# Batch 0's k and v by head halves, two early w_in tiles, and small products joined to the next k times v

## The chip, the cores and the metric

The kernel runs on one core of one Trainium2 chip. The metric is the device time of one execution in microseconds (us); the median of three runs of the kernel before is 1548.06. The core has a matrix engine (TensorE, here PE, with its weight loads PEld), VectorE (DVE), ScalarE (ACT), GpSimd (POOL) and SyncE (SP), whose queue issues nearly all DMAs.

## The reference

Three stages follow each other; q, k, v and the result are f32:

```
kv  = einsum('bhsd,bhse->bhde', k, v)          # 8 batches, 8 heads, 576 rows, head size 64
o   = einsum('bhsd,bhde->bhse', q, kv)
x   = o / sqrt(mean(o*o, -1) + 1e-6) * g_norm  # then (8*576 = 4608 tokens, 512)
x   = (s * relu(x @ w_in1)**2 + b) @ w_out1    # hidden size 2048
h   = x @ w_in2;  out = (h * sigmoid(h)) @ w_out2
```

The weight matrices arrive as f64, which the kernel reads as pairs of 32-bit words and decodes into f32 parts.

## The kernel before

All work is laid out by a planner (class `Plan`, method `run`). Each step is added with a price for each engine that could do it, a key (its due time in units), what it needs, makes, takes and gives, and, for a DMA, its time on the bus (`move`). The planner runs a clock of its own and at each point gives the free engine the ready step with the smallest key; this fixes the order of instructions on each engine for good. On the chip an engine waits for whatever its next instruction needs, and all that stands behind it in its queue waits too. `DMA_START`, `DMA_END` and the rates set how the planner reckons a DMA's landing. A unit is one of the 16 slices of 128 hidden columns of one block of 512 tokens: 12 products into `h` and 12 into `acc`, each 512 columns wide; wide products are made three at a time from high and low halves (`mm3`). Until 40 us of the planner's clock, PE's free time is filled with products of zeros (`warm_up`, line 1321).

A block is a batch's first 512 rows; the 64 remaining rows of the eight batches make a ninth. Attention goes by pairs of heads (`attention_pair(bb, p, key, before)`): 4 pairs in each of 8 batches. `kv` multiplies k by v in one burst of products into one PSUM bank: four chunks of 128 rows and one of 64 remaining rows (in a tile padded with zeros), for each of two heads, with the heads in the two halves of the output's partitions and so in two halves of 64 weight columns. `o` multiplies q by it, `rem` does so for the 64 remaining rows (line 566), `sq` and `part` square and sum in parts, `ms` adds the parts up over partitions on PE (line 640), `rms`, `inv`, `spread` and `x` norm the block. `rem` and `ms` are lone f32 products of 128 weight columns, each in a PSUM bank of its own. The tiles `kv`, `rem`, `q` and `qT` of later batches have one buffer each. `o` of a pair needs the x of the pair before it (`prev`), and the burst needs that pair's remaining rows to be copied out (`prev_r`).

Batch 0 (`z`) borrows the space of weight tiles that are not yet decoded (`wtag`). Its k and v come as 128 partitions of four rows of each head, and the remaining rows of all eight heads in two loads of their own (`load_rem`, 128 KB each, rows of 256 bytes) that the first burst waits for. Its q is turned by products with the identity (`q0_turn`, line 501).

`decode` reads one weight tile (`load`, 512 KB for a whole tile of layer 1) and makes its high and low parts: `mag`, `carry`, `hi` on ACT, `sign`, `top`, `lo` on DVE, `total` on POOL. The first two w_in tiles have keys -5 and -4.8, after all loads of batch 0, whose keys are -15, -13, -11 and -9 by pair.

From line 1303 on the pairs get their keys and are added in the order of them; blocks 1 to 4 are worked in plain units, the rest later in pairs of blocks with seven products in place of eight (`hidden`, `outputs`).

Of the kernel before, what the change touches and what calls it, by code (L numbers as in the profile page):

```python
# [8 lines left out]
F32 = mybir.dt.float32  # L9
# [10 lines left out]
class Plan:  # L20
# [10 lines left out]
    PE_START = 1.1  # L31

# [7 lines left out]
    def add(self, engines, key, fn, needs=(), makes=(), takes=(), gives=(), move=None, opens=(), until=None):  # L40
        self.ops.append((key, len(self.ops), engines, fn, needs, makes, takes, gives, move, opens, until))
        for b in gives:
            self.users[b] = self.users.get(b, 0) + 1

    def run(self):
# [41 lines left out]
        while done < len(self.ops):  # L87
# [46 lines left out]
def kernel(  # L134
# [148 lines left out]
    def decode(layer, kind, m, c, width, sfx, key, needs=(), quarter=None, made=()):  # L283
# [153 lines left out]
    def lend(tag):  # L437
        return f32(wp.tile([P, 2, DM], F32R, tag=tag, name=f"lent_{tag}"))
# [9 lines left out]
    def attention_pair(bb, p, key, before=None):  # L448
# [13 lines left out]
        rr = slice(REM, 2 * REM) if z else slice(REM)  # L462

        def kv_tile(e):
            st["kv"] = lend(wtag["kv"]) if z else ap.tile([P, 2, 2 * T // P * D], F32, tag="kv", name="kv", bufs=1)
# [11 lines left out]
        def load_rem(i):  # L477
            def go(e):
                dst, h = (lent["rem"], slice(0, H)) if z else (rem_t, hh)
                dma(  # L480
                    dst[:REM, i].rearrange("p (h d) -> p h d", d=D), (k, v)[i][bb, h, T:, :].rearrange("h p d -> p h d")
                )
# [12 lines left out]
        def q0_turn(e):  # L495
            lent["z", p] = lend_flat(wtag["qT"], 2 * DM)
            st["psq"] = psum(b["psq"], "q_ps")
            t = st["q"].rearrange("p (h c d) -> p h c d", h=2, d=D)
# [24 lines left out]
        def kv(e):  # L523
            pk = st["psk"] = psum(b["psk"], "kv_ps")
            t = st["kv"].rearrange("p i (h c d) -> p i h c d", h=2, d=D)
            t2 = lent["rem"][:, :, 2 * p * D:2 * (p + 1) * D] if z else rem_t
            for c in range(NCH + 1):
                for j in range(2):
                    jj = slice(j * D, (j + 1) * D)
                    kk = t[:, 0, j, c, :] if c < NCH else t2[:, 0, jj]  # L530
                    vv = t[:, 1, j, c, :] if c < NCH else t2[:, 1, jj]
                    nc.tensor.matmul(pk[jj, :D], kk, vv, start=(c == 0), stop=(c == NCH))  # L532

# [14 lines left out]
        def q0_out(e):  # L548
            copy(e, lent["z", p][:, :T].rearrange("p (t c) -> p t c", t=P), st["psq"].rearrange("p (c t) -> p t c", t=P))
# [36 lines left out]
        fr = (0, 0) if z else me  # L586

        prev, prev_r = ([], []) if z else ([("x32",) + before], [("ro",) + before])
        add({"PE": 0.73}, key, kv, needs=[f("k"), f("v"), ("kr",) + fr, ("vr",) + fr] + prev_r, makes=[f("kv")],
            takes=[b["psk"]], gives=[b["kv"], ("wo12", 0) if z else b["rem"]])  # L590
        add({ACT: 0.21, DVE: 0.26}, key + 0.3, kv_out, needs=[f("kv")] + ([("kvf0L",)] if z else []), makes=[f("kvf")],
            takes=[b["kvf"]], gives=[b["psk"]])
        if z:
            add({"PE": 0.5}, key + 0.2, q0_turn, needs=[f("q")], makes=[f("qt")], takes=[b["psq"], b["qT"]], gives=[b["q"]])
            add({ACT: 0.56}, key + 0.25, q0_out, needs=[f("qt")], makes=[f("q32")], gives=[b["psq"]])
            add({"PE": 0.95}, key + 1.5, o, needs=[f("kvf"), f("q32")], makes=[f("o")], takes=[b["pso"]])
# [13 lines left out]
        add({"PE": 0.2}, key + 2.2, rem, needs=[f("kvf"), f("qT")], makes=[f("r")], takes=[] if z else [b["psr"]],  # L610
            gives=[b["kvf"], b["qT"]])
# [4 lines left out]
        normalize(bb, p, key + 2, [f("o")], [b["pso"]] + [b["qT"]] * z, lambda: st["pso"])  # L616

    def normalize(t, p, key, needs, gives, src):
# [5 lines left out]
        psm = ("at", ("m", me))  # L624
# [13 lines left out]
        def ms(e):  # L638
            st["ps"] = psum(psm, "m_ps")
            nc.tensor.matmul(st["ps"][:, :T // Q], pairs_of, st["part"], start=True, stop=True)  # L640

        def rms(e):
            st["rms"] = ap.tile([P, T // Q], F32, tag="rms", name="rms", bufs=2)
            nc.scalar.activation(st["rms"], st["ps"][:, :T // Q], AF.Sqrt, bias=eps, scale=1.0 / D)
# [20 lines left out]
        add({"PE": 0.2}, key + 0.4, ms, needs=[f("part")], makes=[f("ms")], takes=[psm], gives=[("part", me)])  # L665
# [524 lines left out]
    with tc.manual_schedule():  # L1190
# [8 lines left out]
        lent["rem"] = lend("wo12")  # L1199
        nc.vector.memset(lent["rem"][REM:], 0.0)  # L1200
# [177 lines left out]
```

## Time and profile before

| | us |
|---|---|
| runs | 1549.67, 1547.32, 1548.06 |
| profiled execution | 1549.24 |
| its span | 1547.5 |
| PE busy | 1536.7 |
| granted TensorE clock, mean | 0.998 |

The span is what the trace covers; the execution's time includes some 1.7 us around it. PE is busy nearly throughout, also with the fillers, so its busy time alone does not tell useful work. An f32 product shows as two records; wide products are one record each. The end of a record is modelled and overlaps the next record, so distances between starts are the measure on PE.

### The profile page before, as it was taken

The numbers are of one execution on the slowest core, as the hardware profiler recorded it, in microseconds if no ns is written. First come the engines' busy times: TensorE is split into PE (matmuls) and PEld (weight loads), VectorE is DVE, ScalarE is ACT, GpSimd is POOL, SyncE is SP. The second block draws the span as 40 slices with busy tenths as digits, with TensorE's granted clock in tenths as the row PEclk, the third lists the DMA queues.
The fourth block names the chain that finished last, engine by engine and source line by source line (L and its number), as shares of the span: only waits on it lengthen the run. The fifth ranks groups of instructions, "written<-read, shape, count | busy, mean of one in ns | idle before, by whom it ended". The sixth has DMA issues, their size and how long they took to land.

```text
span 1547.5 us, 23039 instructions
## 1 busy us (share of the span) xinstructions
PE 1536.7 (99%) x7402; PEld 1255.4 (81%) x7402; DVE 1084.1 (70%) x1908; ACT 855.9 (55%) x1683; POOL 634.4 (41%) x584
## 2 busy tenths in 40 slices
PE   9999999999999999999999999999999999999999
PEld 6778888887888888888888788888888888888887
DVE  6887787877677587888888766765676666666521
ACT  6886566566576586667665444544444344544222
POOL 2331122111125144578457823762376246622410
PEclk9999999999999999999999999999999999999999
DMA  8866789988466788897988876877677766876684
GB/s 220 214 188 197 218 253 285 280 233 243 164 217 231 254 254 261 281 310 249 333 277 289 259 239 192 264 189 252 190 258 189 250 196 218 189 254 200 198 197 150
DMA packets 343496, 361.22 MB, mean 233 GB/s; under 512 B 166480, under 2 KB 228944, under 8 KB 343376
## 3 DMA queue, kind: packets, MB, share of 16 engines
q1 hardware_dynamic: 343248, 359.76, 76.4%
q8 instruction: 59, 0.97, 0.3%
q14 instruction: 61, 0.50, 0.1%
q0 software_dynamic: 128, 0.00, 0.0%
HBM read 272.63 MB, written 87.03 MB: 232 GB/s over the span
## 4 chain that ended last, share of the span: by engine, by line
PE 88%; DMA 4%; DVE 3%; ACT 2%; SPq 1%; issue 1%; POOL 1%; POOLq 0%; ACTq 0%; DVEq 0%
PE hp L980 28%; PE acc L1121 10%; PE acc L1123 10%; PE acc L1122 10%; PE h L208 5%; PE h L210 4%; PE h L209 4%; PE acc L208 4%; PE acc L209 4%; PE acc L210 4%; DMA raw<-in_moe_w_out_dram 1%; PE kv_ps L532 1%; PE acc L820 1%; PE acc L819 1%; PE acc L821 1%; SPq L236 1%
## 5 line engine op out<-in xcount | busy, mean ns | idle before, releaser
L980 PE MATMUL hp<-xo,win 128*128 128x512 f32 x2016 | 510.6, 390 | 1.8 <-DVE tmp L1005 1.8
L980 PEld LDWEIGHTS hp<-xo,win 128*128 128x128 f32 x2016 | 378.0, 188 | 84.1 <-DVE tmp L1005 5.9
L220 POOL TENSOR_TENSOR g<-tmp,g 128x512 fp32r<-128x512 f32 x192 | 249.7, 1308 | 309.4 <-ACT g L214 277.7
L1121 PE MATMUL acc<-g,wout 128*128 128x512 f32 x672 | 262.0, 390 | 0.8 <-DVE ya L1132 0.5
L1123 PE MATMUL acc<-g,wout 128*128 128x512 f32 x672 | 261.8, 390 | 0.0
L1122 PE MATMUL acc<-g,wout 128*128 128x512 f32 x672 | 261.7, 389 | 0.0
L1130 DVE TENSOR_TENSOR ya<-acc,ya 128x512 f32<-128x512 f32 x168 | 115.6, 688 | 126.9 <-PE acc L1123 117.8
L1121 PEld LDWEIGHTS acc<-g,wout 128*128 128x128 f32 x672 | 126.1, 188 | 27.9 <-DVE ya L1132 0.9
L1123 PEld LDWEIGHTS acc<-g,wout 128*128 128x128 f32 x672 | 126.3, 188 | 26.4
L1122 PEld LDWEIGHTS acc<-g,wout 128*128 128x128 f32 x672 | 126.3, 188 | 26.2
L214 ACT ACTIVATE g<-tmp 128x512 fp32r<-128x512 f32 x192 | 119.4, 629 | 26.3 <-PE acc L1123 11.7
L208 PE MATMUL acc<-gh,wo 128*128 128x512 f32 x320 | 132.2, 413 | 0.4 <-ACT y L227 0.4
L786 ACT ACTIVATE h<-h 128x512 f32<-128x512 f32 x96 | 56.0, 583 | 131.9 <-PE h L210 131.3
L208 PE MATMUL h<-xh,wi 128*128 128x512 f32 x320 | 126.7, 396 | 0.1
L1157 POOL TENSOR_TENSOR ya<-ya 128x512 f32<-128x512 f32 x84 | 108.2, 1318 | 45.1 <-DVE ya L1130 35.6
L210 PE MATMUL h<-xh,wi 128*128 128x512 f32 x320 | 125.2, 391 | 0.0
L210 PE MATMUL acc<-gh,wo 128*128 128x512 f32 x320 | 125.2, 391 | 0.0
L209 PE MATMUL acc<-gh,wo 128*128 128x512 f32 x320 | 125.1, 391 | 0.0
L209 PE MATMUL h<-xl,wi 128*128 128x512 f32 x320 | 124.9, 390 | 0.0
L332 POOL TENSOR_TENSOR rq<-raw 128x256 uint32<-128x256 uint32 x68 | 43.5, 640 | 189.5 <-DVE raw L318 101.1
L1005 DVE TENSOR_TENSOR tmp<-hp,tmp 128x512 f32<-128x512 f32 x144 | 98.8, 686 | 24.5 <-PE hp L980 23.1
L214 ACT ACTIVATE rq<-rq 128x256 fp32r<-128x256 f32 x192 | 77.5, 413 | 63.4 <-POOL rq L332 28.9
(170 smaller groups left out, 2649.4 us busy)
## 6 DMA issues: line engine op xcount, KB each, us to landing
wout<-wo SPq DMA_DIRECT2D x368, 256.0 KB, 4.2
win<-wi SPq DMA_DIRECT2D x144, 512.0 KB, 5.1
wi<-rq SPq DMA_DIRECT2D x96, 256.0 KB, 3.7
wo<-rq SPq DMA_DIRECT2D x96, 256.0 KB, 3.4
win<-wi SPq DMA_DIRECT2D x80, 256.0 KB, 4.2
raw<-in_moe_w_out_dram SPq DMA_DIRECT2D x36, 256.0 KB, 4.2
raw<-in_moe_w_in_dram SPq DMA_DIRECT2D x16, 512.0 KB, 4.8
raw<-in_moe_w_in_dram SPq DMA_DIRECT2D x32, 256.0 KB, 4.8
```

Of the source, the lines that this page charges most:

```text
L208: nc.tensor.matmul(ps, wh, xh, start=first, stop=False)
L209: nc.tensor.matmul(ps, wh, xl, start=False, stop=False)
L210: nc.tensor.matmul(ps, wl, xh, start=False, stop=last)
L214: nc.scalar.activation(hi, src, AF.Copy)
L220: eng[e].tensor_tensor(lo, src, f32(hi), op=ALU.subtract)
L980: nc.tensor.matmul(to, w[:, wn, f_], x_[:, xn], start=first and n == 0, stop=kk == KH - 1 and n == 2, skip_group_check=True)
L1005: nc.vector.tensor_tensor(t, bank[me, a], tmp[b_, me], op=ALU.add)
L1121: nc.tensor.matmul(to, w[:, 0, dd], gh, start=a == 0, stop=False)
L1122: nc.tensor.matmul(to, w[:, 0, dd], gl, start=False, stop=False)
L1123: nc.tensor.matmul(to, w[:, 1, dd], gh, start=False, stop=a == 1)
L1130: nc.vector.tensor_tensor(y2[tp, i, d], st["ps"], y2[tp, i, d], op=ALU.add)
L1157: eng[e].tensor_tensor(y2[tp, i, d], y2[tp, i, d], y2[tp, j, d], op=ALU.add)
```

## The change

It does five things. (1) Batch 0's k and v are loaded with a head in 64 partitions, nine rows in each, so the remaining rows come with them and `load_rem` is gone for batch 0; its burst becomes nine chunks of 64 rows for each head. Its q is loaded in the same way (eight rows in a partition) and turned in 16 products of 64 columns in place of 8 of 128. (2) The loads of the first two w_in tiles get keys -13.5 and -11.5. (3) For later pairs `rem` and `ms` are no longer steps: `kv` of the next pair issues them at its end, each as two products of 64 weight columns, into columns 64 to 143 of its own bank. The burst now needs the pair's `kvf`, `qT` and `part`. The last pair and batch 0 keep the lone form. (4) Pairs of batches 2 to 4 get other keys. (5) The planner reckons DMAs that are issued before 9 us at 1.2 times their length and with 1.8 us at the end, and some steps have other prices.

```diff
+    EARLY, EARLY_RATE, EARLY_END = 9.0, 1.2, 1.8
...
-                dma = max(dma, end + self.DMA_START) + op[8] * (self.BUSY_RATE if busy else 1.0)
-                end = dma + (self.DMA_BUSY if busy else self.DMA_END)
+                early = end < self.EARLY
+                dma = max(dma, end + self.DMA_START) + op[8] * (self.BUSY_RATE if busy else self.EARLY_RATE if early else 1.0)
+                end = dma + (self.DMA_BUSY if busy else self.EARLY_END if early else self.DMA_END)
...
-        first = layer == 0 and (kind, m) == ("i", 0)
-        add({"SP": 0.48}, -5 if first else key - 5 - 0.8 * (layer == 0 and (kind, m) == ("i", 1)), load, needs=needs, makes=[f(0)], takes=[raw], move=width * P * 8 / 3.6e5)
-        key -= 0.5 if first else 0.5
+        add({"SP": 0.48}, {(0, "i", 0): -13.5, (0, "i", 1): -11.5, (0, "o", 0): -3.4}.get((layer, kind, m), key - 5), load, needs=needs, makes=[f(0)], takes=[raw], move=width * P * 8 / 3.6e5)
+        key -= 0.5
...
+    bursts, joined = {}, {}
+
+    def attention_pair(bb, p, key, before=None, after=None):
...
-        wtag = {"kv": f"wo{8 + p}", "q": f"wo{4 + p}", "qT": f"wi{11 + p}", "kvf": "kvf0L"}
+        wtag = {"kv": f"wo{8 + p}", "v": f"wi{9 - p}", "q": f"wo{4 + p}", "qT": f"wi{11 + p}", "kvf": "kvf0L"}
         b = {n: (wtag[n] if z else n, me) for n in ("kv", "rem", "q", "qT") if not (z and n == "rem")}
+        if z:
+            b["v"] = (wtag["v"], me)
...
+        host = ("at", ("k", after)) if after else None
+        if after:
+            b["psr"] = host
+        rr = slice(REM, 2 * REM) if z or after else slice(REM)
...
+        def load_rows(i):
+            def go(e):
+                t = st["kv"[i]] = lend_flat(wtag[("kv", "v")[i]], S)
+                dma(t, (k, v)[i][bb, hh].rearrange("h (p c) d -> (h p) (c d)", p=D))
+            return go
...
-            st["q"] = lend_flat(wtag["q"], 2 * T // P * D)
-            dma(
-                st["q"].rearrange("p (h c d) -> p h c d", h=2, d=D), q[bb, hh, :T, :].rearrange("h (p c) d -> p h c d", p=P)
-            )
+            st["q"] = lend_flat(wtag["q"], T)
+            dma(st["q"], q[bb, hh, :T, :].rearrange("h (p c) d -> h p (c d)", p=D))
...
-            for c in range(NCH):
+            for c in range(T // D):
+                cc = slice(c * D, (c + 1) * D)
                 for j in range(2):
-                    nc.tensor.matmul(st["psq"][j * D:(j + 1) * D, c * P:(c + 1) * P], t[:, j, c, :], ident, start=True, stop=True)
+                    jj = slice(j * D, (j + 1) * D)
+                    nc.tensor.matmul(st["psq"][jj, cc], st["q"][jj, cc], ident[jj, jj], start=True, stop=True)
...
+            if z:
+                n = S // D
+                for c in range(n):
+                    cc = slice(c * D, (c + 1) * D)
+                    for j in range(2):
+                        jj = slice(j * D, (j + 1) * D)
+                        nc.tensor.matmul(pk[jj, :D], st["k"][jj, cc], st["v"][jj, cc], start=(c == 0), stop=(c == n - 1))
+                return
...
+            bursts[me] = pk
+            for more in joined.get(before, ()):
+                more()
...
+            if after:
+                st["psr"] = bursts[after]
+                for jj in (slice(D), slice(D, P)):
+                    nc.tensor.matmul(st["psr"][jj, rr], st["kvf"][:, jj], st["qT"][:, T:], start=True, stop=True)
+                return
...
-        add({"SP": 0.48}, lk, load(0), makes=[f("k")], opens=[f("kvo")], takes=[b["kv"]], move=0.73)
-        add({"SP": 0.48}, lk, load(1), needs=[f("kvo")], makes=[f("v")], move=0.73)
-        if not z or p == 0:
-            rb = ("wo12", 0) if z else b["rem"]
-            add({"SP": 0.63}, lk, load_rem(0), makes=[f("kr")], opens=[f("remo")], takes=[rb], move=0.73 if z else 0.18)
-            add({"SP": 0.63}, lk, load_rem(1), needs=[f("remo")], makes=[f("vr")], move=0.73 if z else 0.18)
+        if z:
+            for i in range(2):
+                add({"SP": 0.48}, lk, load_rows(i), makes=[f("kv"[i])], takes=[b[("kv", "v")[i]]], move=0.82)
+        else:
+            add({"SP": 0.48}, lk, load(0), makes=[f("k")], opens=[f("kvo")], takes=[b["kv"]], move=0.73)
+            add({"SP": 0.48}, lk, load(1), needs=[f("kvo")], makes=[f("v")], move=0.73)
+            add({"SP": 0.63}, lk, load_rem(0), makes=[f("kr")], opens=[f("remo")], takes=[b["rem"]], move=0.18)
+            add({"SP": 0.63}, lk, load_rem(1), needs=[f("remo")], makes=[f("vr")], move=0.18)
...
-        add({"PE": 0.73}, key, kv, needs=[f("k"), f("v"), ("kr",) + fr, ("vr",) + fr] + prev_r, makes=[f("kv")],
-            takes=[b["psk"]], gives=[b["kv"], ("wo12", 0) if z else b["rem"]])
+        more = before in joined
+        if more:
+            prev_r = [(x,) + before for x in ("kvf", "qT", "part")]
+        add({"PE": 1.2 if z else 0.93 + 0.24 * more}, key, kv, needs=[f("k"), f("v")] + ([] if z else [f("kr"), f("vr")]) + prev_r,
+            makes=[f("kv")] + ([(x,) + before for x in ("r", "ms")] if more else []), takes=[b["psk"]],
+            gives=[b["kv"], b["v"] if z else b["rem"]] + ([(f"kvf{before[1] % 2}", before), ("qT", before), ("part", before)] if more else []))
...
+            add({"PE": 1.0}, key + 0.2, q0_turn, needs=[f("q")], makes=[f("qt")], takes=[b["psq"], b["qT"]], gives=[b["q"]])
...
+            add({"PE": 1.1}, key + 1.5, o, needs=[f("kvf"), f("q32")], makes=[f("o")], takes=[b["pso"]])
...
-        add({"PE": 0.2}, key + 2.2, rem, needs=[f("kvf"), f("qT")], makes=[f("r")], takes=[] if z else [b["psr"]],
-            gives=[b["kvf"], b["qT"]])
+        if after:
+            joined[me] = [lambda: rem("PE")]
+        else:
+            add({"PE": 0.25}, key + 2.2, rem, needs=[f("kvf"), f("qT")], makes=[f("r")], takes=[] if z else [b["psr"]],
+                gives=[b["kvf"], b["qT"]])
...
+        psm = ("at", ("k", after) if after else ("m", me))
+        mc = slice(P, P + T // Q) if after else slice(T // Q)
...
+            if after:
+                st["ps"] = bursts[after]
+                for jj in (slice(D), slice(D, P)):
+                    nc.tensor.matmul(st["ps"][jj, mc], pairs_of[:, jj], st["part"], start=True, stop=True)
+                return
...
-        add({"PE": 0.2}, key + 0.4, ms, needs=[f("part")], makes=[f("ms")], takes=[psm], gives=[("part", me)])
+        if after:
+            joined[me].append(lambda: ms("PE"))
+        else:
+            add({"PE": 0.23}, key + 0.4, ms, needs=[f("part")], makes=[f("ms")], takes=[psm], gives=[("part", me)])
...
-        lent["rem"] = lend("wo12")
-        nc.vector.memset(lent["rem"][REM:], 0.0)
...
-        seq = [(t, p, KF * (t - 1) + (0.5 + (3.2 if t < LB else 2.0) * p if t > 1 else 0.75 + 3.4 * p)) for t in range(1, TP) for p in range(NP)]
+        seq = [(t, p, KF * (t - 1) + (-2 + (3.7 if t < LB else 2.0) * p if t > 1 else 0.75 + 3.4 * p)) for t in range(1, TP) for p in range(NP)]
...
-        for t, p, key in sorted(seq, key=lambda c: c[2]):
-            attention_pair(t, p, key, before)
+        seq.sort(key=lambda c: c[2])
+        for n, (t, p, key) in enumerate(seq):
+            attention_pair(t, p, key, before, seq[n + 1][:2] if n + 1 < len(seq) else None)
```

## Rows read from the trace of the kernel before

**Rows 1.** The page, busy us (share of the span) xinstructions of each engine

```profile
PE 1536.7 (99%) x7402; PEld 1255.4 (81%) x7402; DVE 1084.1 (70%) x1908; ACT 855.9 (55%) x1683; POOL 634.4 (41%) x584
```

**Rows 2.** Windows: length; PE, PEld, DVE, ACT, POOL busy (records); clock, DMA share, GB/s

```profile
0.00:27.00 27.00, 24.55 (x252) 18.26 (x253) 14.05 (x36) 13.47 (x32) 5.45 (x15) 1.00 0.91 237
...
45.00:430.00 385.00, 383.23 (x2173) 308.78 (x2171) 300.33 (x630) 255.00 (x569) 84.45 (x104) 1.00 0.77 227
...
840.00:880.00 40.00, 37.58 (x157) 29.96 (x156) 30.29 (x49) 18.31 (x37) 33.22 (x32) 0.96 0.82 262
```

**Rows 3.** Windows of line L1321, the fillers: PE and PEld busy (xrecords)

```profile
0.00:27.00 27.00, 13.14 (x91) 9.72 (x91) 1.00 0.91 237
27.00:45.00 18.00, 5.49 (x41) 3.27 (x39) 1.00 0.75 196
```

**Rows 4.** Timeline of PE at a k times v burst: start, us, what

```profile
121.08 0.39 PE L210 MATMUL acc<-gh,wo 128*128 128x512 f32 x1
121.40 0.69 PE L532 MATMUL kv_ps<-kv 128*64 128x64 f32 x16
121.92 0.29 PE L532 MATMUL kv_ps<-rem_t 128*64 128x64 f32 x4
...
122.47 0.39 PE L209 MATMUL acc<-gh,wo 128*128 128x512 f32 x1
```

**Rows 5.** Timeline of PE at a product for the remaining rows

```profile
69.74 0.39 PE L210 MATMUL h<-xh,wi 128*128 128x512 f32 x1
69.97 0.33 PE L566 MATMUL r_ps<-qT,kvf 128*128 128x64 f32 x2
...
70.42 0.40 PE L209 MATMUL acc<-gh,wo 128*128 128x512 f32 x1
```

**Rows 6.** Timeline of PE at a product for the mean squares

```profile
140.24 0.39 PE L210 MATMUL h<-xh,wi 128*128 128x512 f32 x1
140.47 0.29 PE L640 MATMUL m_ps<-part,pairs_of 128*128 128x16 f32 x2
140.61 0.50 PE L208 MATMUL h<-xh,wi 128*128 128x512 f32 x1
140.94 0.40 PE L209 MATMUL h<-xl,wi 128*128 128x512 f32 x1
```

**Rows 7.** Lines of PE: remaining rows of later pairs, xrecords | busy, mean ns

```profile
L566 PE MATMUL r_ps<-qT,kvf 128*128 128x64 f32 x56 | 9.3, 247 | 0.0
```

**Rows 8.** Timeline of all engines, 289 to 296 us: one later pair's chain

```profile
289.44 0.29 PE L640 MATMUL m_ps<-part,pairs_of 128*128 128x16 f32 x2
...
292.08 0.74 DVE L659 SCALAR_TENSOR_TENSOR x<-o_ps,vecs,sq 128x512 f32<-128x512 f32 x1
...
295.39 0.70 DVE L633 TRANSPOSE_TENSOR_REDUCE part<-sq 128x16 f32<-128x512 f32 x1
```

**Rows 9.** Waits of PE, 45 to 430 us: total, times, longest

```profile
PE m_ps L640 <- DVE orem L233: 0.8, 2, 0.6
```

**Rows 10.** Timeline of PE in the start

```profile
5.65 0.97 PE L532 MATMUL kv_ps<-lent_wo 128*64 128x64 f32 x16
7.76 0.34 PE L532 MATMUL kv_ps<-lent_wo 128*64 128x64 f32 x4 [1.14 <-DMA lent_wo<-in_v_dram]
...
18.33 1.09 PE L501 MATMUL q_ps<-ident,lent_wo 128*64 128x128 f32 x16
```

**Rows 11.** Windows in the start, columns as in rows 2

```profile
3.00:8.00 5.00, 3.86 (x33) 2.64 (x31) 0.83 (x5) 0.00 (x0) 2.16 (x8) 1.00 0.77 203
...
14.00:19.00 5.00, 5.00 (x59) 3.30 (x57) 3.06 (x6) 3.41 (x11) 0.00 (x0) 1.00 1.09 348
...
15.70:31.00 15.30, 15.30 (x134) 11.79 (x133) 14.38 (x29) 11.90 (x25) 2.40 (x2) 1.00 0.90 228
```

**Rows 12.** Timeline of DVE: a decode pass, pair 3's x

```profile
22.26 0.66 DVE L318 SCALAR_TENSOR_TENSOR raw<-dw,raw 128x512 uint32<-128x512 uint32 x1
...
29.92 0.69 DVE L220 TENSOR_TENSOR xl<-x,xh 128x512 fp32r<-128x512 f32 x1 [0.35 <-ACT xh L214]
```

More of the change, by code (lines that the diff above doesn't have):

```diff
@@ L446 @@
     lent = {}
-    def attention_pair(bb, p, key, before=None):
+    bursts, joined = {}, {}
+    def attention_pair(bb, p, key, before=None, after=None):
         me = (bb, p)
@@ L461, in attention_pair @@
         b["psq"] = ("acc", ("q", me))
-        rr = slice(REM, 2 * REM) if z else slice(REM)
+        host = ("at", ("k", after)) if after else None
+        if after:
+            b["psr"] = host
+        rr = slice(REM, 2 * REM) if z or after else slice(REM)
         def kv_tile(e):
-            st["kv"] = lend(wtag["kv"]) if z else ap.tile([P, 2, 2 * T // P * D], F32, tag="kv", name="kv", bufs=1)
+            st["kv"] = ap.tile([P, 2, 2 * T // P * D], F32, tag="kv", name="kv", bufs=1)
+        def load_rows(i):
[3 more added lines that the diff above has]
+            return go
         def load(i):
@@ L478, in go @@
             def go(e):
-                dst, h = (lent["rem"], slice(0, H)) if z else (rem_t, hh)
                 dma(
-                    dst[:REM, i].rearrange("p (h d) -> p h d", d=D), (k, v)[i][bb, h, T:, :].rearrange("h p d -> p h d")
+                    rem_t[:REM, i].rearrange("p (h d) -> p h d", d=D), (k, v)[i][bb, hh, T:, :].rearrange("h p d -> p h d")
                 )
@@ L497, in q0_turn @@
             st["psq"] = psum(b["psq"], "q_ps")
-            t = st["q"].rearrange("p (h c d) -> p h c d", h=2, d=D)
-            for c in range(NCH):
+            for c in range(T // D):
+                cc = slice(c * D, (c + 1) * D)
                 for j in range(2):
-                    nc.tensor.matmul(st["psq"][j * D:(j + 1) * D, c * P:(c + 1) * P], t[:, j, c, :], ident, start=True, stop=True)
+                    jj = slice(j * D, (j + 1) * D)
+                    nc.tensor.matmul(st["psq"][jj, cc], st["q"][jj, cc], ident[jj, jj], start=True, stop=True)
         def q0_rem_turn(e):
@@ L524, in kv @@
             pk = st["psk"] = psum(b["psk"], "kv_ps")
+            if z:
[6 more added lines that the diff above has]
+                return
             t = st["kv"].rearrange("p i (h c d) -> p i h c d", h=2, d=D)
-            t2 = lent["rem"][:, :, 2 * p * D:2 * (p + 1) * D] if z else rem_t
             for c in range(NCH + 1):
@@ L529, in kv @@
                     jj = slice(j * D, (j + 1) * D)
-                    kk = t[:, 0, j, c, :] if c < NCH else t2[:, 0, jj]
-                    vv = t[:, 1, j, c, :] if c < NCH else t2[:, 1, jj]
+                    kk = t[:, 0, j, c, :] if c < NCH else rem_t[:, 0, jj]
+                    vv = t[:, 1, j, c, :] if c < NCH else rem_t[:, 1, jj]
                     nc.tensor.matmul(pk[jj, :D], kk, vv, start=(c == 0), stop=(c == NCH))
+            bursts[me] = pk
+            for more in joined.get(before, ()):
+                more()
         def kv_out(e):
@@ L548, in q0_out @@
         def q0_out(e):
-            copy(e, lent["z", p][:, :T].rearrange("p (t c) -> p t c", t=P), st["psq"].rearrange("p (c t) -> p t c", t=P))
+            copy(e, lent["z", p][:, :T].rearrange("p (t c) -> p t c", t=D), st["psq"].rearrange("p (c t) -> p t c", t=D))
         def q_hi(e):
@@ L585, in attention_pair @@
                 opens=[f("qo")] * (i == 0), takes=[b["q"]] * (i == 0), move=0.42)
-        fr = (0, 0) if z else me
         prev, prev_r = ([], []) if z else ([("x32",) + before], [("ro",) + before])
-        add({"PE": 0.73}, key, kv, needs=[f("k"), f("v"), ("kr",) + fr, ("vr",) + fr] + prev_r, makes=[f("kv")],
-            takes=[b["psk"]], gives=[b["kv"], ("wo12", 0) if z else b["rem"]])
+        more = before in joined
[4 more added lines that the diff above has]
+            gives=[b["kv"], b["v"] if z else b["rem"]] + ([(f"kvf{before[1] % 2}", before), ("qT", before), ("part", before)] if more else []))
         add({ACT: 0.21, DVE: 0.26}, key + 0.3, kv_out, needs=[f("kv")] + ([("kvf0L",)] if z else []), makes=[f("kvf")],
@@ L593, in attention_pair @@
         if z:
-            add({"PE": 0.5}, key + 0.2, q0_turn, needs=[f("q")], makes=[f("qt")], takes=[b["psq"], b["qT"]], gives=[b["q"]])
+            add({"PE": 1.0}, key + 0.2, q0_turn, needs=[f("q")], makes=[f("qt")], takes=[b["psq"], b["qT"]], gives=[b["q"]])
             add({ACT: 0.56}, key + 0.25, q0_out, needs=[f("qt")], makes=[f("q32")], gives=[b["psq"]])
-            add({"PE": 0.95}, key + 1.5, o, needs=[f("kvf"), f("q32")], makes=[f("o")], takes=[b["pso"]])
+            add({"PE": 1.1}, key + 1.5, o, needs=[f("kvf"), f("q32")], makes=[f("o")], takes=[b["pso"]])
             add({"PE": 0.2}, key + 2.1, q0_rem_turn, needs=[("qr0",), f("kvf"), ("mm1o", 1, KD - 1)], makes=[f("qrt")], takes=[b["psr"]], gives=[("wo13", 0)])
@@ L615, in attention_pair, with normalize @@
             makes=[f("orem")], gives=[b["orem"]], move=0.18)
-        normalize(bb, p, key + 2, [f("o")], [b["pso"]] + [b["qT"]] * z, lambda: st["pso"])
-    def normalize(t, p, key, needs, gives, src):
+        normalize(bb, p, key + 2, [f("o")], [b["pso"]] + [b["qT"]] * z, lambda: st["pso"], after)
+    def normalize(t, p, key, needs, gives, src, after=None):
         z = t == 0
@@ L623, in normalize @@
         f = lambda name: (name, t, p)
-        psm = ("at", ("m", me))
+        psm = ("at", ("k", after) if after else ("m", me))
+        mc = slice(P, P + T // Q) if after else slice(T // Q)
         def sq(e):
@@ L638, in ms @@
         def ms(e):
+            if after:
[3 more added lines that the diff above has]
+                return
             st["ps"] = psum(psm, "m_ps")
-            nc.tensor.matmul(st["ps"][:, :T // Q], pairs_of, st["part"], start=True, stop=True)
+            nc.tensor.matmul(st["ps"][:, mc], pairs_of, st["part"], start=True, stop=True)
         def rms(e):
             st["rms"] = ap.tile([P, T // Q], F32, tag="rms", name="rms", bufs=2)
-            nc.scalar.activation(st["rms"], st["ps"][:, :T // Q], AF.Sqrt, bias=eps, scale=1.0 / D)
+            nc.scalar.activation(st["rms"], st["ps"][:, mc], AF.Sqrt, bias=eps, scale=1.0 / D)
         def inv(e):
```

## Prediction

> **What bounds the kernel now.** I read the page's busy times first. The matrix engine (PE) is busy 99% of the span [rows 1], so an edit pays only if it takes time out of PE's own queue or brings PE's first useful product forward. The windows by stage [rows 2] show where that is possible. Up to 27 us PE shows 24.55 us of busy time, but the group of the zero products [rows 3] shows that 13.14 us of it are fillers, and 5.49 us of the next 18: this start waits for data. From 45 to 430 us, where the 28 later head pairs are worked, PE is busy 383.23 of 385 us without fillers: there each PE instruction removed is time removed. After 430 us nothing of the change is at work. The one large loss there is between 840 and 880 us (37.58 of 40 busy at a granted clock of 0.96, [rows 2]), in layer 2's preparation.
>
> **The joined products.** In the main stream products of 512 columns start 0.227 us apart. I measure an insertion from the start of the product before it to the start of the second product after it, less two such steps (0.454).
> - A k times v burst: 121.08 to 122.47 is 1.39, so it costs 0.94 us [rows 4]. It starts 0.32 us after its predecessor instead of 0.227: entering the form in two halves of 64 columns costs 0.09. It has 20 records (each f32 product shows as two), whose 0.52 us from 121.40 to 121.92 for the first 16 records gives 0.065 us for two records; I take 0.06.
> - The product for the 64 remaining rows: 69.74 to 70.42 is 0.68, so 0.23 us [rows 5].
> - The product for the mean squares: 140.24 to 140.94 is 0.70, so 0.25 us [rows 6].
> Both are two records; nearly all of their price is entering and leaving the other kind of product, since the next wide product starts 0.33 us before its successor instead of 0.227 [rows 6]. The change issues each as two halves, four records, inside a burst that has already paid for entering. Four pairs of records at 0.06 us make 0.24 us. So each joined head pair saves 0.23 + 0.25 - 0.24 = 0.24 us. 28 later pairs exist (the remaining rows' product shows 56 records for them [rows 7], two for each); all but the last have a successor, so 27 x 0.24 = 6.5 us go. No trace shows these halves with a 16-column right side: below, they cost nothing and 27 x 0.48 = 13 us go; above, every record runs alone (8 x 0.06 = 0.48) and nothing goes. I take 6.5, since the halves of the burst itself are the nearest row, and both have the same 64-column weights.
>
> What waits instead: the next burst now needs the partial sums of the pair before, and the transposed q (one buffer) is free only after that burst. Behind a burst that waits stands all of PE's queue. In the dense stretch mean squares at 289.44 led to x ending at 292.82 (3.4 us), and the next partial sums ended at 296.10, 3.3 us later [rows 8]. A cycle is thus some 6.9 us with the burst's own 0.2. 24 pairs lie between units 14 and 52; a unit is 24 wide products (5.4 us) and some 0.7 us for the pairs, so they are about 9.7 us apart; where two keys coincide (21.4 and 21.5, 37.4 and 37.5) the planner must spread them. So I expect no regular stall. The waits that PE has now on the mean squares are 0.8 us behind the vector engine (DVE) [rows 9]; some come back at the bursts, so I book -0.3. The moved keys (-2 instead of 0.5 units) start later pairs sooner and cost nothing on PE.
>
> **The start.** Batch 0's k and v no longer bring the remaining rows apart. Now the first burst began at 5.65 us with its first 16 records, and its last four waited until 7.76 for those rows [rows 10]. While they were under way the DMA moved 203 GB/s (3 to 8 us) against 348 later (14 to 19 us) [rows 11]: 5 x (1 - 203/348) = 2.1 us lost, which go. Their bytes stay (256 KB, now inside k and v). The two w_in tiles (512 KB, 1.5 us each at 348 GB/s) are issued in SP's queue ahead of pairs 1 to 3 and of pairs 2 and 3, ten and seven loads. Pair 0 gains 2.1 us, pair 1 gains 0.6, pairs 2 and 3 lose 0.9; the whole group ends 2.1 us earlier, and so do the loads queued behind it (the first later pair, then w_out's first tile). On PE, batch 0's burst has 36 records instead of 20, 18 x 0.06 = 1.1 us; the q turn has 32 records, about 1 us as now. If 64-row halves do not run side by side, each takes 1 us more for every pair. The fillers hide these, except for pair 3's own turn.
>
> The decode of the two tiles runs on ScalarE, DVE and POOL. DVE was busy 14.38 us of the 15.3 from 15.7 to 31 [rows 11], with both tiles and four pairs in it. A tile costs it three passes; the one at 22.26 took 0.66 us [rows 12], and I take 1.7 us a tile, 3.4 for two. These now fall before the dense stretch, where DVE is mostly idle. PE's turn for pair 3 started at 18.33 [rows 10] and the low half of its x ended at 30.61 [rows 12], 12.3 us. With 3 us less on DVE's list I put that at 9.3. When does that turn start? Its q lands 0.9 us later than now, though PE came to it only after other work. The planner also holds it back: it now counts early loads at 1.2 times their length and 0.7 us more at the end, so its last q lands at 1.2 + 1.2 x 12.8 + 1.8 = 18.3 of its clock instead of 12.9, and fillers are laid by that clock. I take 18.5. So x is whole at 27.8 instead of 30.6, and the first unit's fourth product, which waits for it, comes 2.8 us earlier. The next steps (w_out's first tile, the second unit) are served by loads that are 2.1 us earlier and by a DVE with less to do. I book -2.8; bounds are +1 (the turn 0.9 us later, as its q, and no shorter list) and -5 (the turn 1.5 us sooner than I take it and 0.7 us less behind it). The cleared rows that DVE wrote at the very start go too; DVE waits there, so they are worth nothing.
>
> The Trainium skill (TensorEngine Tiling, Restrictions and Gotchas) says that different row tiles cannot use one PSUM bank at the same time. By that, batch 0's halves, which now differ in rows and share a bank, would take turns: the start would give 0.8 us instead of 2.8 and the sum would be 2 us higher. No run here has row halves; the burst's halves of today differ in columns alone.
>
> **Sum.** The profiled execution took 1549.24 us (span 1547.5 and 1.74 around it), 1.18 above the median of 1548.06. 1549.24 - 6.5 - 0.3 - 2.8 = 1539.6; taken back to the median, 1538.4 us. Its own range is 1532 (start -5, all waits gone, part of the loss at 840 us gone) to 1544 (start +1, 1.5 us of new waits).
>
> **Rivals.**
> 1. The start gives nothing. The planner's later landings lay more fillers, and ScalarE's decode is the limit in the ramp up to 45 us. For: PE never ran ahead of the fillers after 10 us. Against: the ramp still holds 5.49 us of fillers [rows 3], and 3.4 us of DVE's work have left it. Time: 1538.4 + 2.8 = 1541.2.
> 2. The bursts wait. If a third of the 27 found the partial sums 0.7 us late, 6 us return: 1544.5. For: PE waited on the mean squares before, and the burst now stands on two chains of some 3.4 us in a row. Against: 6.9 us of cycle in 9.7 us.
> 3. Slower: batch 0's q loads run on few DMA engines. Their source now has the head (2) as its outermost dimension. If only two of 16 engines carry it, 256 KB at 2/16 of 348 GB/s takes 6.0 us instead of 0.75; four loads add 21 us, and what is queued behind on these two engines waits as well. Pair 3's turn would start near 39 and x end near 48, 17 us late. Of that the fillers up to 45 us return about 5.5 and the joined products 6.8, so 1549.24 + 17 - 5.5 - 6.8 - 1.2 = 1552.8. It decides from about 4 us a q load on. For: q alone is not contiguous over both heads, so its two heads cannot merge into 128 rows as k's and v's do. Against: no load of the kernel before has such a form, so no row shows that it is slow; its other side still has 128 partitions.
>    The Trainium skill (DMA: Bandwidth & Descriptors, Why a DMA increments its semaphore by 16 and not by 1) says that the number of engines is the largest up to 16 that divides the outermost sizes of both sides, here 2. By that rule this rival would be the forecast; no run here shows it, since every load of the kernel before has a multiple of 16 outermost.
> 4. The loss at 840 to 880 us goes with the changed order: another 4 us, 1534.5. The order there comes from the same keys as now, so this is chance alone.
>
> **Chances.** Forecast 0.50, rival 1 0.17, rival 2 0.09, rival 3 0.16, rival 4 0.08. About 0.2% (3.1 us) can be told from no change, so faster is below 1545.0 and slower above 1551.2. Faster: 0.49 + 0.16 + 0.05 + 0.08 = 0.78. Slower: rival 3 but for its mildest part, 0.15. The rest, 0.07, is the same. For 8 in 10 the range runs from 1531 to 1549: it leaves out most of rival 3 and the far end of rival 4. The case of my forecast alone is 1532 to 1544.
>
> **What would show it.** Joined: between 45 and 400 us no lone product for remaining rows or mean squares stands between wide products; a burst takes some 1.17 us by the measure above; the bursts have few waits. Start: the first burst is whole by about 6.7 us, the decode of the first w_in tile starts before 10 us, the product that waits for pair 3's x starts by 28.5. Wrong: a q load that takes over 4 us longer than k and v beside it (rival 3); over 3 us of PE waits at the bursts (rival 2); the fourth product still near 30 us with the tiles long decoded (rival 1).

## The result and the profile after

The changed kernel took 1565.23 us (median of 4 runs, 1562.22 to 1566.57), the kernel before 1548.87 (4 runs, 1547.32 to 1550.17): a ratio of 1.0102 [1.0088, 1.0116]. It is 16.4 us slower where 10 us less were forecast, and outside the forecast range. The profiled execution took 1566.57 us with a span of 1564.8, 17.3 more than the span of before.

The page's busy line, answering to [rows 1], and the windows that answer to [rows 2]:

```profile
PE 1532.7 (98%) x7602; PEld 1252.4 (80%) x7602; DVE 1073.6 (69%) x1881; ACT 852.2 (54%) x1693; POOL 649.7 (42%) x600
```

```profile
0.00:27.00 27.00, 17.14 (x218) 12.36 (x218) 8.27 (x22) 8.62 (x19) 5.20 (x16) 0.81 0.52 151
45.00:430.00 385.00, 375.04 (x2291) 302.13 (x2292) 294.74 (x599) 258.37 (x589) 102.82 (x121) 1.00 0.79 228
840.00:880.00 40.00, 39.52 (x175) 32.37 (x174) 34.50 (x55) 21.94 (x42) 32.64 (x29) 1.00 0.82 269
```

In the first 27 us the granted clock is 0.81 of full speed in place of 1.00, the DMA moves 151 GB/s in place of 237, and PE is busy 7.4 us less. That is where the loss arises. PE's waits up to 57 us name what was late:

```profile
PE q_ps L513 <- DMA lent_wo<-in_q_dram: 14.2, 4, 6.7
PE h L210 <- ACT xh L216: 1.6, 1, 1.6
```

PE stood 14.2 us for the q of batch 0, once for each of the four pairs. The timeline of PE shows where (start, us, what, and the idle time before it); [rows 10] has the turn of pair 3 at 18.33:

```profile
4.98 1.26 PE L543 MATMUL kv_ps<-lent_wi,lent_wo 64*64 64x64 f32 x36
12.90 1.97 PE L513 MATMUL q_ps<-ident,lent_wo 64*64 64x64 f32 x32 [6.66 <-DMA lent_wo<-in_q_dram]
...
21.52 1.15 PE L513 MATMUL q_ps<-ident,lent_wo 64*64 64x64 f32 x32 [1.36 <-DMA lent_wo<-in_q_dram]
...
31.34 1.97 PE L513 MATMUL q_ps<-ident,lent_wo 64*64 64x64 f32 x32 [4.52 <-DMA lent_wo<-in_q_dram]
...
39.23 1.15 PE L513 MATMUL q_ps<-ident,lent_wo 64*64 64x64 f32 x32 [1.65 <-DMA lent_wo<-in_q_dram]
...
53.00 0.49 PE L210 MATMUL h<-xh,wi 128*128 128x512 f32 x1 [1.60 <-ACT xh L216]
```

The first burst was whole at 6.24 (6.7 was forecast), but the turn behind it started at 12.90. The first product that needs pair 3's x (wide products come in groups of three, and it opens the first unit's fourth group) started at 53.00; before it was at 30.39. The DMA view over the first 45 us has a row of GB/s in 40 slices of 1.125 us, first of the kernel before, then of the changed one:

```profile
GB/s 0 33 314 182 153 121 282 368 357 351 290 181 300 353 340 353 345 298 130 72 74 73 357 371 292 306 33 198 316 162 173 320 0 33 175 313 160 328 52 282
```

```profile
GB/s 0 70 307 158 103 231 301 275 113 46 48 141 352 214 132 270 50 49 46 143 37 40 134 370 85 48 46 111 344 110 65 106 119 45 33 81 92 180 291 344
```

Between 8 and 20 us the kernel before moves 290 to 368 GB/s nearly throughout. The changed one falls again and again to 46 to 50. Two sixteenths of 348 [rows 11] are 43.5. A window inside one of these stretches shows that two of the sixteen DMA engines are at work, since their mean busy share (the last number but one) is 0.13, and 2/16 is 0.125:

```profile
10.20:11.80 1.60, 0.00 (x0) 0.00 (x0) 0.00 (x0) 0.00 (x0) 0.00 (x0) 0.50 0.13 48
```

They carry a q load, and nothing else is moving. Why nothing else moves is seen in SP's timeline, where most issues take 0.4 to 0.7 us:

```profile
1.19 0.42 SPq L238 DMA_DIRECT2D lent_wi<-in_v_dram  x1
...
4.32 2.50 SPq L238 DMA_DIRECT2D lent_wi<-in_v_dram  x1
...
7.47 4.34 SPq L238 DMA_DIRECT2D raw<-in_moe_w_in_dram  x1
...
16.02 4.85 SPq L238 DMA_DIRECT2D lent_wo<-in_q_dram  x2
20.91 3.53 SPq L238 DMA_DIRECT2D lent_wo<-in_k_dram  x1
```

Behind the q loads several single issues take 2.5 to 4.3 us, so the loads after them are asked for late. (A long issue alone does not prove such a load: in q_old, a run below without it, one took 3.00 us.) And PE's waits cost more than their length, as two windows of the changed kernel show (the last three numbers: granted clock, DMA share, GB/s):

```profile
13.00:19.00 6.00, 6.00 (x48) 3.94 (x50) 2.41 (x6) 2.17 (x5) 1.04 (x1) 0.54 0.69 204
...
29.00:36.00 7.00, 4.66 (x40) 3.76 (x40) 1.74 (x4) 1.33 (x3) 0.00 (x0) 0.53 0.45 127
```

With the idle stretches of 6.66 and 4.52 us the clock fell to its lower level, 1.2 GHz, and PE began its next work there: the turns at 12.90 and 31.34 took 1.97 us where at full clock one took 1.15.

The joined burst itself came as forecast. PE at one of them, answering to [rows 4 to 6]:

```profile
117.32 0.39 PE L212 MATMUL acc<-gh,wo 128*128 128x512 f32 x1
117.64 0.69 PE L551 MATMUL kv_ps<-kv 128*64 128x64 f32 x16
118.15 0.29 PE L551 MATMUL kv_ps<-rem_t 128*64 128x64 f32 x4
118.27 0.29 PE L589 MATMUL kv_ps<-qT,kvf 128*64 128x64 f32 x4
118.39 0.25 PE L678 MATMUL kv_ps<-part,pairs_of 128*64 128x16 f32 x4
118.56 0.50 PE L210 MATMUL acc<-gh,wo 128*128 128x512 f32 x1
118.90 0.39 PE L211 MATMUL acc<-gh,wo 128*128 128x512 f32 x1
```

117.32 to 118.90 less 0.454 is 1.13 us (1.17 was forecast), 0.19 over the plain burst of before, so with the prediction's prices of the lone products a pair saves 0.29 us on PE, and 27 of them 7.8.

### The profile page after: what moved, and what is told of

Read it like the earlier page. It is cut to its first block, busy times and chain, and to the rows that moved or that the text cites. A ratio compares the mean times of both kernels' runs of the same rounds, so it can differ in the third digit from the quotient of the medians.

```text
span 1564.8 us, 23436 instructions
## 1 busy us (share of the span) xinstructions
PE 1532.7 (98%) x7602; PEld 1252.4 (80%) x7602; DVE 1073.6 (69%) x1881; ACT 852.2 (54%) x1693; POOL 649.7 (42%) x600
## 4 chain that ended last, share of the span: by engine, by line
PE 83%; DMA 7%; DVE 4%; SPq 3%; issue 1%; ACT 1%; POOL 1%; DVEq 0%; POOLq 0%; ACTq 0%
PE hp L1024 28%; PE acc L1165 9%; PE acc L1167 9%; PE acc L1166 9%; PE h L210 4%; PE h L211 4%; PE h L212 4%; PE acc L210 3%; PE acc L211 3%; PE acc L212 3%; SPq L238 3%; DMA raw<-in_moe_w_in_dram 2%; DMA wo<-rq 1%; PE acc L865 1%; PE acc L863 1%
## 5 line engine op out<-in xcount | busy, mean ns | idle before, releaser
L216 ACT ACTIVATE g<-tmp 128x512 fp32r<-128x512 f32 x192 | 119.4, 629 | 26.1 <-PE acc L1167 11.5
```

The lines of the kernel that those rows point to most:

```text
L216: nc.scalar.activation(hi, src, AF.Copy)
```

## The experiments

The theory after the result, A: the load of q with its two heads outermost, alone, costs the 20 us of the start; without it the change is near the forecast. The rivals were other parts of the start (the w_in tiles, the k and v halves, the tiny loads) and the joining. The before of each run is the kernel before in the same comparison (1548.2 to 1549.2 us).

How late a kernel is at some point of its work can be read from its wide products, which are the same 6336 in every kernel. The table has how many us later than in the kernel before the 24th starts (the last into the `h` of the first two units: the start is over), the 1921st (the first of the pairs of blocks: the stretch with the joined products is over) and the 3401st and 3601st (around the loss at 840 to 880 us). Each row is one profiled execution.

| | 24th | 1921st | 3401st | 3601st |
|---|---|---|---|---|
| changed kernel | 20.4 | 19.6 | 19.9 | 17.2 |
| q_alone | 18.6 | 23.0 | 22.9 | 20.0 |
| q_old | 2.1 | -1.8 | -1.7 | -4.7 |
| q_two | 6.8 | 4.7 | 5.0 | 2.1 |
| vecs_late | 4.3 | -2.2 | -1.9 | -4.8 |
| join_only | 2.1 | 0.7 | 0.8 | -0.8 |
| join_keys | 0.7 | -2.4 | 3.9 | 1.0 |
| no_join | 5.5 | 10.4 | 10.4 | 7.5 |

**Only the q load and its turn, on the kernel before** (q_alone):

```diff
-st["q"].rearrange("p (h c d) -> p h c d"), q[bb, hh, :T, :].rearrange("h (p c) d -> p h c d", p=P)
+st["q"], q[bb, hh, :T, :].rearrange("h (p c) d -> h p (c d)", p=D)
```

> The kernel before, with the new load of batch 0's q alone (and its turn in 16 products that goes with it); k, v, w_in, the later pairs and the planner's reckoning as before. Theory A: four loads of 6 us in place of 0.75, so 15 to 22 us slower, 1564 to 1571 us. Rival B: within 2 us of the kernel before.

1568.52 us, 1.0125 [1.0109, 1.0142], 19.4 us more than before. Its waits of PE up to 57 us:

```profile
PE q_ps L500 <- DMA lent_wo<-in_q_dram: 12.6, 4, 5.2
```

The same four waits stand in a kernel that has nothing else of the change.

**The changed kernel with q loaded and turned as before** (q_old, the same lines the other way):

> The changed kernel with batch 0's q loaded and turned as before (128 partitions, rows of 1 KB); all else as changed. If the q loads by heads into 64 partitions cost more than one load into 128 (0.5 us each for 128 KB against 0.75 for 256 KB), this is 1 to 3 us faster than the variant with two q loads, 1549 to 1551. If what is left of the loss comes from the w_in tiles or from k and v (theories E and F), within 1 us of it.

1544.87, 0.9978 [0.9968, 0.9987]: 20.4 us less than the change as given, and below what was expected. From both sides the first half of theory A stands. The second half does not: without the q load the change is 6.5 us above the forecast.

**The q load split by head, 64 partitions outermost** (q_two), **and the same with 4 outermost** (q_four):

```diff
-dma(st["q"], q[bb, hh, :T, :].rearrange("h (p c) d -> h p (c d)", p=D))
+for j in range(2):   # q_two
+    dma(st["q"][j * D:(j + 1) * D], q[bb, 2 * p + j, :T, :].rearrange("(p c) d -> p (c d)", p=D))
+# q_four: ....rearrange("(b a c) d -> a b (c d)", a=4, b=16), undone in the copy after the turn
```

> The changed kernel, but batch 0's q comes in two loads for each pair, one for each head, so that 64 partitions are the outermost dimension of both sides; the bytes and the rows in a partition stay. Theory A (a q load whose source has the 2 heads outermost is carried by two DMA engines, 47 GB/s, and holds up all loads behind it): the q loads land within 1 us of k and v, the waits of PE on q go from 14.2 us to under 1, the fourth product of the first unit starts near 28 us instead of 53, and the time is 1541 us (1536 to 1546). Rival B (the loss comes from the w_in tiles that were put ahead, or from the planner's later reckoning): the time stays above 1558 us.

> As the variant with two q loads for each pair, but each load's source walks its rows so that an outermost dimension of 4 is left (16 inside it); the turned q is put back in order when it is copied out. Theory A (the outermost size sets the number of DMA engines): a load of 128 KB at 4 of 16 engines takes 1.5 us instead of 0.4, 3 us a pair, so the stretches with q loads alone show about 90 GB/s, and the time lies 4 to 9 us above the variant with two loads. Rival C (what counts is whether the load walks both heads, or the size of its rows): same time as the variant with two loads, within 2 us.

q_two: 1551.96, 1.0017 [1.0008, 1.0027]; 13.3 of the 20 us come back, fewer than theory A expected (1541). q_four: 1552.04, 1.0021 [1.0006, 1.0037]. The medians do not tell 4 from 64 outermost, against what was expected. The engines do: in q_four, from 20.0 to 21.5 us, the mean busy share is 0.27 at 99 GB/s, so four of sixteen carry its q loads, as theory A had it.

```profile
20.00:21.50 1.50, 1.50 (x11) 0.67 (x8) 1.37 (x5) 1.50 (x5) 0.00 (x0) 1.00 0.27 99
```

What that costs in time is not shown. In the profiled execution PE waited for q 5.8 us in q_four and 1.7 us in q_two, but that execution of q_four (1556.62) was the second slowest of its ten. Two loads cost 7 us more than the one of before: pair 3 is turned at 26.27 in q_two and at 23.17 in q_old, and q_two's PE ran a burst and a turn at the lower clock after a wait:

```profile
13.74 2.04 PE L544 MATMUL kv_ps<-lent_wi,lent_wo 64*64 64x64 f32 x36 [2.13 <-DMA lent_wi<-in_v_dram]
15.50 1.99 PE L514 MATMUL q_ps<-ident,lent_wo 64*64 64x64 f32 x32
```

**The w_in tiles asked for as late as before**, on q_two (win_late) and on q_old (q_old_win):

```diff
-{(0, "i", 0): -13.5, (0, "i", 1): -11.5, (0, "o", 0): -3.4}.get((layer, kind, m), key - 5)
+{(0, "i", 0): -5, (0, "i", 1): -4.8}.get((layer, kind, m), key - 5)
```

> The variant with two q loads, but the first two w_in tiles keep their keys of before, behind batch 0's loads. Theory E (the two tiles of 512 KB put ahead push pairs 2 and 3 back, and these decide): the last q lands by 20 us instead of 24.25 and the time is 1541 to 1546 us. Rival F (k and v by head halves come more slowly, 1.2 us for 288 KB where 256 KB took 0.75): 1549 to 1552 us.

> The changed kernel with q loaded and turned as before, and with the two w_in tiles asked for as late as before: what is left of the start's change is k and v by halves. Theory I (two w_in tiles ahead put pairs 1 to 3 some 3 us back on the bus, and this eats what VectorE's shorter list gives): q of pair 3 is turned near 18.5 us in place of 23.2 of the kernel with early w_in and old q, and the 13th wide product stands within 1 us of that kernel's; by time 1544 to 1547, no clear difference. Theory J (the early tiles do give VectorE its room): 1547 to 1550, the 13th wide product 2 us or more later.

win_late: 1549.61, 1.0005 [0.9992, 1.0019], 2.4 us below q_two, in rival F's range and above theory E's. q_old_win: 1546.05, 0.9985 [0.9975, 0.9994], not to be told from q_old. So in time the early tiles are worth nothing, as theory I had it. The profile shows the trade; pair 3's turn and products that open a group of three, in q_old_win (the tenth and the 13th wide product) and then in q_old (the 13th and the 19th):

```profile
18.61 1.09 PE L514 MATMUL q_ps<-ident,lent_wo 128*64 128x128 f32 x16
...
31.48 0.50 PE L210 MATMUL h<-xh,wi 128*128 128x512 f32 x1 [0.85 <-ACT wi L216]
...
32.54 0.40 PE L210 MATMUL h<-xh,wi 128*128 128x512 f32 x1
```

```profile
23.17 1.09 PE L514 MATMUL q_ps<-ident,lent_wo 128*64 128x128 f32 x16
...
29.59 0.48 PE L210 MATMUL h<-xh,wi 128*128 128x512 f32 x1
...
34.32 0.50 PE L210 MATMUL h<-xh,wi 128*128 128x512 f32 x1 [0.35 <-ACT xh L216]
```

With late tiles the turn is at 18.61 (18.5 was expected); the product at 31.48 waits for the second w_in tile's decode, and the first one that needs pair 3's x comes at 32.54, 13.9 us behind the turn. With early tiles the turn is 4.6 us later and that product, at 34.32, 11.2 us behind it. So the early tiles shorten the way behind the turn and delay the turn by more. The 13th wide product, which theory I wanted within 1 us, starts 2.95 us later with late tiles, as theory J had it; by the 24th (35.19 against 36.46) late tiles are ahead. What k and v by halves are worth has no run of its own; q_old_win against join_only below (0.9985 and 0.9977) shows no gain from them.

**The joining alone** (join_only: the kernel before with the joined products, their prices and the new keys of batches 2 to 4), **the same with the keys of before** (join_keys), **and q_two without joining and new keys** (no_join):

```diff
-attention_pair(t, p, key, before)                                             # join_only
+attention_pair(t, p, key, before, seq[n + 1][:2] if n + 1 < len(seq) else None)
-(-2 + (3.7 if t < LB else 2.0) * p if t > 1 ...)                              # join_keys
+(0.5 + (3.2 if t < LB else 2.0) * p if t > 1 ...)
```

> The kernel before with the joined small products alone (with their keys and prices); batch 0, the w_in tiles and the planner's reckoning as before. If joining is worth what the variant without it lost (8.2 us), this takes 1541 us (1538 to 1544), and PE's stretch from 45 to 430 us of before is done 7 to 9 us sooner. Rival D (it only made up for a late start there): 1546 to 1550 us.

> The kernel before with the joined small products and their prices, but the keys of batches 2 to 4 as before. Theory M (joining alone is the gain): 1543 to 1547, as with the new keys (1545.0). Theory N (the burst that now waits for the pair's parts needs the new keys): 1547 to 1553, with waits on the accumulating pair's part ahead of bursts of over 3 us in sum that the kernel with new keys does not have.

> As the variant with two q loads for each pair, but later pairs keep their lone products for the remaining rows and the mean squares, with the keys of before. If a joined pair saves 0.24 us on PE and brings no new waits, this is 6.8 us slower than the variant with two loads (5 to 9). Rival D (the bursts wait for what the lone products waited for): within 2 us of it.

join_only: 1544.97, 0.9977 [0.9965, 0.999], 4.1 us gained, less than the 1538 to 1544 expected. join_keys: 1548.25, 1.0002 [0.9993, 1.0012], nothing gained. no_join: 1560.2, 1.007 [1.0055, 1.0086], 8.2 above q_two. So joining and keys together are worth 4 to 8 us, and on the kernel before joining with the old keys gains nothing in time. No run has the new keys without joining, so what the keys do by themselves is not shown. The mechanism that theory N gave is not what the profiles show. PE's waits from 45 to 440 us, of join_only and then of join_keys:

```profile
PE kv_ps L671 <- DVE part L662: 3.2, 3, 1.7
```

```profile
PE kv_ps L671 <- DVE part L662: 0.7, 1, 0.7
```

The bursts waited less with the old keys, and from the 24th to the 1921st product join_keys gained 3.1 us and join_only 1.4 (its profiled execution, 1548.64, is the slowest of its ten). The profiled execution of join_keys lost its time from 535 to 790 us, in the pairs of blocks (waits of PE, then the window):

```profile
PE hp L1017 <- DVE tmp L1042: 4.5, 3, 2.3
```

```profile
535.00:790.00 255.00, 250.46 (x1095) 205.87 (x1094) 212.31 (x356) 171.60 (x334) 143.74 (x136) 0.99 0.85 279
```

join_only has 254.79 us of PE there, as the kernel before has. How the keys of batches 2 to 4 reach so far, and whether other executions lose time there, is not settled.

**The four tiny loads (s, b, g_norm) issued after pair 0's k times v**, on q_two (vecs_late), on q_old (q_old_vecs) and on the kernel before (before_vecs): a step of POOL in the plan in place of four issues at the top.

```diff
-nc.gpsimd.dma_start(out=s_t, ...)   # and b_t, g0 twice, ahead of the plan
+add({POOL: 2.4}, -8, small, needs=[("kvf", 0, 0)], makes=[("small",)], move=0.1)
```

> The variant with two q loads, but the four tiny loads of GpSimd's queue (s, b and g_norm, elements of 4 bytes) are issued only when pair 0's k times v is copied out. Theory G (they slow all loads beside them from 4 to 7 us, not the 256-byte rows that the prediction blamed): that stretch shows over 250 GB/s instead of some 130, the loads behind land 1.5 us earlier, and the time is 1 to 2 us less, 1550 to 1551. Rival H: the stretch stays under 200 GB/s and the time the same.

> The changed kernel with q loaded and turned as before, and the four tiny loads of s, b and g_norm issued only after the first kv product is copied out. Theory K (the tiny loads slow the first loads, whichever these are; they gave 7 us back in the kernel with two q loads): 1539 to 1543, all loads of batch 0 landing 1.5 us or more earlier than with the tiny loads first. Theory L (they gave back only what the clock lost in a wait that two q loads made): 1544 to 1547.

> The kernel before with only the four tiny loads of s, b and g_norm issued after the first kv product is copied out. Theory K (they slow the first loads): 1543 to 1547 in place of 1549, with a wait of less than 1.1 us for v ahead of the first burst's last four records. Theory L: 1548 to 1551.

vecs_late: 1545.02, 0.998 [0.997, 0.999], 7 us below q_two, more than either theory expected. q_old_vecs: 1546.63, 0.9986 [0.9978, 0.9995], no gain over q_old. before_vecs: 1552.43, 1.003 [1.0019, 1.0041], slower; PE waited 2.14 us there for the v of pair 0 where [rows 10] has 1.14. From 4 to 7 us vecs_late moved 103 GB/s, where theory G expected over 250 and q_two had 133. So theories G and K fall: no gain from later tiny loads repeats. What gave 7 us in the one case is open; by the table about a third of it is there at the 24th product, and the rest comes between the 24th and the 1921st.

No version is clearly the best: q_old, join_only and vecs_late lie at 1545, 0.2% below the kernel before.

## Why the prediction was wrong

**The step that failed** is the q load. The sum booked it at 0.75 us like the load of before ("pairs 2 and 3 lose 0.9") and put the other outcome aside as rival 3, at a chance of 0.16, because "no load of the kernel before has such a form, so no row shows that it is slow". That no row shows it was no evidence for its being cheap. In its place the runs showed a load on two of sixteen engines, at 46 to 50 GB/s of 348, although the other side has 128 partitions; alone it costs 19.4 us (q_alone) or 20.4 (the changed kernel against q_old). By the Trainium skill (DMA: Bandwidth & Descriptors, Why a DMA increments its semaphore by 16 and not by 1) two engines carry a load of this form, and the trace agrees (a mean busy share of 0.13).

**Rival 3's own time** was 1552.8, 12.4 too low. Its turn of pair 3 "near 39" came at 39.23. But x was to be whole 9 us later and the product that needs it came 13.8 us later: ACT had the decode of a w_in tile queued ahead of pair 3's x, and that tile's load landed at 51.2, as ACT's timeline shows:

```profile
51.21 0.67 ACT L311 ACTIVATE dw<-raw 128x512 f32<-128x512 f32 x1 [0.79 <-DMA raw<-in_moe_w_in_dram]
51.77 0.66 ACT L328 ACTIVATE raw<-raw 128x512 uint32<-128x512 uint32 x1
52.32 0.63 ACT L216 ACTIVATE xh<-x 128x512 fp32r<-128x512 f32 x1
```

And the fillers gave nothing back: their number is laid down in the order (81 records ahead of the 24th wide product, in the changed kernel as in q_old), so they ran all the same behind the late loads. The 24th wide product started at 54.76 in place of 34.36, 20.4 us late.

**The joined products.** Forecast -6.8 with their waits. In the changed kernel the 1921st wide product was still 19.6 us late, so they gave 0.8. The price was nearly right (0.29 a pair at the burst above, 0.24 forecast); what ate it were waits (rival 2 in part). PE's waits from 57 to 555 us, where before had 1.5 us of them from 36 to 535:

```profile
PE o_ps L211 <- DVE qTl L222: 1.9, 3, 1.3
PE acc L210 <- ACT gh L218: 1.7, 1, 1.7
PE kv_ps L551 <- DMA kv<-in_v_dram: 1.3, 1, 1.3
PE kv_ps L678 <- DVE part L669: 1.1, 3, 0.4
```

All waits there sum to 7.6 us, 6 more than before, and behind the one on gh products stood 0.43 us apart for 2 us, the lower clock again (granted 0.76 from 77 to 84 us):

```profile
79.39 0.50 PE L210 MATMUL acc<-gh,wo 128*128 128x512 f32 x1 [1.67 <-ACT gh L218]
80.43 0.80 PE L211 MATMUL acc<-gh,wo 128*128 128x512 f32 x1 [0.54 <-DVE gh L224]
...
81.88 0.63 PE L211 MATMUL h<-xl,wi 128*128 128x512 f32 x1
82.31 0.63 PE L212 MATMUL h<-xh,wi 128*128 128x512 f32 x1
```

Only the waits on part are on the edge that the change added. A late start costs in this stretch without any joining: q_alone, which joins nothing, loses 4.4 us there (18.6 to 23.0 in the table). So a part of what the joined products gave went to the late start; that the stages ran closer together behind it is argued, not shown. With the q load of before, in q_old, whose profiled execution is at its median, the stretch gained 3.9 us, with these waits on part:

```profile
PE kv_ps L679 <- DVE part L670: 3.1, 5, 1.3
```

**The start without the q load.** Forecast -2.8; q_old against join_only gives none (0.9978 and 0.9977), and in q_old's profile the 24th product is 2.1 us later than before. Two terms failed. The 2.1 us that the remaining rows' loads were to have cost at 3 to 8 us did not come back: without them, and with the q load of before, the same window of q_old reads

```profile
3.00:8.00 5.00, 4.26 (x62) 3.18 (x60) 0.83 (x5) 0.41 (x2) 2.15 (x8) 1.00 0.66 210
```

against 203 [rows 11], so taking them away did not mend the slow beginning. And DVE's list was not 3.4 us shorter to any use: in q_old the two passes of a later w_in tile stood on ACT ahead of pair 3's x (32.46 and 33.04, then xh at 33.61), and turn to product went from 12.1 to 11.2 us in place of 9.3.

**What was right**: batch 0's 64 by 64 halves are no slower in one bank than the column halves of before (36 records in 1.26 us at 18.89, 0.035 each, where the old form took 0.80 for 20, 0.040). The 2 us more that the prediction named by the Trainium skill's rule (TensorEngine Tiling (Array Packing), Restrictions and Gotchas) were not paid.

**What came by luck.** The loss at 840 to 880 us shrank, as in rival 4: the lag fell there from 19.9 to 17.2 us. But that needs no changed order: q_alone, whose order is that of the kernel before, makes up some 3 us at the same place, and all 13 other profiled executions here lose 1.6 to 3.0 us less there than the one of before. PE's waits from 800 to 930 us, before and then in q_alone:

```profile
PE hp L980 <- DVE tmp L1005: 1.6, 1, 1.6
```

```profile
PE hp L979 <- DVE tmp L1004: 0.2, 1, 0.2
```

Why that one execution of before waited is open.

**The sum.** Start, joined products, the way to 840 us, the loss there: 20.4 - 0.8 + 0.3 - 2.7 = 17.2, the difference of the spans but for 0.1.

## What to carry to other kernels

Of every load whose form changes, ask first how its outermost dimension splits over the DMA engines (2 gave two engines here, 4 gave four); a form that no row shows is to be priced at its worst case before it is called free, and here such a load also held back the issues behind it. A cheaper instruction is worth its price only where its new operands are there early: in q_old 3.1 of 7.8 us went to waits for them. Fillers and orders that are laid down in advance give no time back when a load is late.

## What the runs showed that was not expected

- Behind 256 KB loads on two engines several of SP's issues took 2.5 to 4.3 us, where most take 0.4 to 0.7.
- Waits of 6.7 and 4.5 us on PE went with granted clocks of 0.54 and 0.53 in the windows behind and around them. In q_two a wait of 2.13 us was followed by a burst at the lower clock (2.04 us); in q_old one of 2.62 us was not (1.26 us).
- A late start grows: q_alone is 18.6 us late behind its start and 23.0 us late 1900 wide products further on, though nothing there was changed.
- Ten or more executions of one kernel spread over 4 to 9 us here, far more than the 2 us that three runs of before had shown, so that parts worth under 2 us were not told apart.
